# Masks and identity made on GpSimd, and a new order of steps, in a fused linear-attention and gated-MLP kernel

## The chip, the cores and the metric

The kernel runs on one core of one Trainium2 chip. The metric is the device time of one launch in microseconds (us), as the median of the runs shown. TensorE is called PE here, VectorE DVE, ScalarE ACT, GpSimd POOL, and SyncE SP; SP issues every transfer of this kernel.

## The reference

Gated linear attention over 768 tokens for 4 batches of 8 heads of 48 features, followed by a block with a spatial gating unit:

```python
f = 1.0 / (1.0 + np.exp(-f_logit))
for t in range(S):
    state = f[:, :, t, :, None] * state + np.einsum('bhd,bhe->bhde', k[:, :, t], v[:, :, t])
    y[:, :, t] = np.einsum('bhd,bhde->bhe', q[:, :, t], state)
x = y with the heads side by side                      # (4, 768, 384)
h = gelu_tanh(x @ w_in);  u, v = halves of h           # 512 columns each
v_n = (v - mean) / sqrt(var + 1e-6) * g_ln
v_s = np.einsum('ts,bsd->btd', w_sg, v_n) + b_sg[None, :, None]
out = x + (u * v_s) @ w_out
```

## The kernel before

The 3,072 tokens are 24 tiles of 128, six to a batch; three tiles are a group. Every step of a tile has a name and an engine, and a table, ORDER, lists all steps in one sequence. A name with `:DVE`, `:ACT` or `:POOL` behind it is put on that engine; without it the step goes to the first engine of its entry in T (line 41). The class Plan (line 148) walks ORDER with its own costs and sorts the steps by the start that it works out. The program is then written out in that sequence, and each engine runs its own steps in it, strictly one after the other.

The steps that the texts below name, for tile n:

- Loads on SP's queue: `f`, `q`, `k`, `v` (192 KB each), `ldin c` (384 KB of w_in, chunk c of 8), `cs` (the constants, 160 KB). At most eight loads are under way: each later one waits for the landing of the load eight before it.
- Gates: `e` and `l` (ACT, exp and log of f), `cum` (PE, a product with the triangle `tril` of the tile cs), `up` and `dn` (ACT, exp of plus and minus its result), `mq` and `mk` (q and k times these).
- Transposes: `tr` (PE, with `ident` of the tile cs), `tc n.0` and `tc n.1` (copies out of PSUM). `do`, `di`: the decays picked out and copied.
- Attention: `su` (PE, scores and state updates), `ms` (DVE, scores times `mask` of the tile cs), `sa` and `sm` (state added and multiplied), `w` (v shifted by 64 rows), `y` (PE), `ty` and `jy` (y out of PSUM and summed).
- The block: `xT` (PE, x transposed), `xh`, `xl` (its high and low parts), `hv` (PE, the v half of x @ w_in, which reads chunks 4 to 7), `hu` (PE, the u half, chunks 0 to 3), `gv`, `ns`, `nd`, `nq`, `nr`, `nh`, `nl` (the norm), `sg` (PE, the product with w_sg over six tiles), `po` (PE, w_out).
- A chunk of w_in comes as 64-bit floats and is turned into a high and a low part in eight steps: `wa` (ACT), `wp`, `wq`, `wr`, `wc` (DVE), `wd` (their sum), `we` (high part), `wf` (low part). `wd` and `wf` run on DVE or POOL.

POOL starts with `clear` (line 338), which sets the padding columns of the buffers for q, k and the decays. In the idle time that Plan expects on PE up to 45 us it places products of zeros (line 1042), which nothing reads.

Of the kernel before, what the change touches and what calls it, by code (L numbers as in the profile page):

```python
# [18 lines left out]
C = 64
# [48 lines left out]
wqin1 wcin6 mq0 mk0 wrin1 tr0 do0 cum1 tc0.0 tc0.1:DVE w0.1 wcin1 di0 wdin1 up1 dn1 wein1 wain4 w0.0:ACT mq1 su0 ms0
mk1 wdin6 wpin4 wqin4 wrin4 sa0.0 sm0.0 sa0.1 do1 tr1 y0 ldin7 f2 v1 f3 ldin5 q2 k2 f4 q3 f5 v2 k3 tc1.1 wein6 tc1.0
wain7 sm0.1 wcin4 di1 wpin7 ty0 e2 l2 w1.1 jy0 wqin7 su1 xT0 cum2 e3 l3 wain5 xh0 up2 dn2 sa1.0 ms1 wrin7 w1.0 wcin7  # L70
wpin5 wdin7 mq2 xl0 mk2 wfin1:POOL wfin6:POOL wdin4:POOL sm1.0:POOL cum3 y1 do2 tr2 up3 dn3 wein7 ty1 e4 di2:ACT l4
tc2.1 tc2.0 wfin7:POOL one sa1.1 jy1 wqin5 mq3 wein4:DVE wrin5 ldin0 g v3 ldsg2 ldsg1 q4 ldin2 b k4 xT1 cum4 do3 su2
xh1 e5 wcin5 l5 di3 wdin5 xl1 mk3 cum5 tr3 wein5 up4 dn4 wfin5 up5 dn5 tc3.0 w2.0:ACT tc3.1 wain0 ms2 sm1.1 sa2.0
sm2.0 sa2.1 wpin0 wqin0 sm2.1 wrin0 wcin0 w2.1:ACT wfin4:POOL hv1 su3 y2 wT2.0 wT1.0 hv0 gv1 ty2 wh2.0 sa3.0 ns1 ms3
jy2 xT2 wh1.0 nd1 wain2 nq1 xh2 wl1.0 wl2.0 mk4 wpin2 wdin0:POOL sm3.0:POOL sa3.1 xl2 mq4:POOL nr1 gv0 v4 q5 k5 f6
ldsg0 ldin3 v5 bb0 do4 tr4 ns0 wein0:DVE bc0 di4 nh1 tc4.0 tc4.1 w3.1:POOL nl1 mq5 w3.0 wqin2 wT2.1 hv2 y3 su4 wh2.1
nd0:DVE w4.0:ACT gv2 e6 ty3 mk5 wl2.1 wrin2 sm3.1 wcin2 ns2 sa4.0 ms4 w4.1:POOL sm4.0:POOL wdin2:POOL tr5 wT0.0 do5
jy3 sa4.1 sm4.1:POOL w5.1:POOL tc5.1 tc5.0:DVE wain3 wh0.0 xT3 y4 su5 wT0.1 wl0.0 wpin3 w5.0 xh3 wein2 ty4 nd2 wh0.1
nq2 nq0 wqin3 jy4 wfin2 di5 xl3 sa5.0 wrin3 wl0.1 cum_c ms5 hu0.1 xT4 l6 xh4 nr2 sm5.0:POOL wcin3 xl4 sz6 nr0 hu0.2
bb1 y5 hv3 ldout3 q7 ldout1 v7 q6 k6 ldout2 v6 f7 ldsg4 k7 v8 k8 f8 waout1 waout3 bc1 nh0 wpout3 wpout1 lh6:DVE wqout1  # L80
wdin3 nl0 ty5 gu0.1 gu0.2 gv3 jy5 wfin0:POOL wqout3 wrout1 ns3 wcout1 wein3:DVE wdout1 weout1:DVE wrout3 xT5 hu0.0 hv4
wT1.1 xh5 nd3 nq3 nh2 ll6:POOL xl5 nl2 wcout3 nr3 zr waout2 nh3 w6.0:ACT wdout3 hv5 nl3 wpout2 gv4 gu0.0 wh1.1 gv5
w8.0:ACT wfin3 ns4 wl1.1 ns5 nd5:DVE wfout1 wqout2 wrout2 nd4 nq4 nq5 nr4 nr5 hu1.1 cum6 hu1.2 hu1.0 gu1.1 gu1.2
wcout2 nh4:DVE nl4 nh5:DVE wdout2:POOL nl5 hu0.3 hu1.3 up6 dn6 e7 e8 mq6:POOL mk6 tt6.0 weout3 weout2 l7 tt6.1 wfout3
lh7:DVE wfout2:POOL ll7 gu1.3 gu0.3 gu1.0 sg0.0 ldsg3 ldsg5 q8 f9 to6 do6 ti6.0 ti6.1 ti6.3 ti6.2 ldout0 di6.0 di6.1
f10 cum7 wT4.0 wT3.0 sb0.0 e9 l8 up7 l9 wh4.0 wh3.0 dn7 sm_0.0:POOL mq7:POOL wl4.0 wl3.0 sg0.2 wT4.1 wT3.1 sg0.3 lh8
wh3.1 wh4.1 sb0.2 mk7 wl3.1 wl4.1 tt7.0 sm_0.2:POOL ll8:POOL tt7.1 tc6.1:DVE sh0.2:DVE tc6.0 cum8 wT5.1 wT5.0 su6
sl0.2 sb0.3 wh5.0 wh5.1 up8 sh0.0:DVE sm_0.3 lh9:DVE dn8 e10 w6.1:ACT waout0 ll9:POOL mk8:POOL wl5.1 sa6.0 wl5.0
wpout0 wqout0 mq8 do7 to7 f11 ti7.1 ti7.0 di7.1 q9 k9 ti7.2 ti7.3 sg0.1 cum9 sg1.2 sg1.0 sb0.1 wrout0 sm6.0 tt8.0
wcout0 tt8.1 sl0.0 sm_0.1:POOL e11 sh0.1 up9 l10 dn9 lh10:DVE sl0.1 w7.0 wdout0 weout0 ms6 w7.1:POOL ll10:POOL  # L90
sh0.3:DVE sa6.1 tc7.1 tc7.0 sl0.3 mq9 sb1.0 mk9 wfout0:POOL cum10 y6 su7 po1 po0 to8 do8 f12 di7.0 ti8.1 ti8.2 ti8.3
k10 ti8.0 v9 tt9.0 up10 l11 e12 ty6 dn10 sm6.1:POOL jy6 tt9.1 sa7.0 sb1.2 ms7 sm7.0:POOL sm_1.0 sa7.1 mk10 re0 w9.1
lh11:DVE sm7.1:POOL ll11 tc8.1 tc8.0 xT6 y7 su8 po2 cum11 do9 to9 di8.1 q10 di8.0 out0 ti9.3 ti9.0 ti9.2 ti9.1 ty7 xh6
xl6 ms8 jy7 sm_1.2 sa8.0 w8.1:POOL re1 sm8.0 mq10 sa8.1 tt10.0 tt10.1 sh1.2:DVE sh1.0:DVE up11 dn11 tc9.1 tc9.0 sl1.2
di9.1 v10 q11 k11 do10 f13 hv6 y8 su9 xT7 sg1.1 w10.1:ACT l12 ty8 xh7 jy8 xl7 mk11 gv6 lh12 sm8.1:POOL mq11:POOL re2
tt11.0 ns6 tt11.1 ll12:POOL to10 v11 di9.0 out1 f14 ti10.2 ti10.1 do11 ti10.3 ti10.0 to11 di10.1 k12 q12 xT8 sg1.3
cum12 xh8 e13 w10.0:ACT l13 lh13 up12 e14 ms9 sa9.0 xl8 sb1.1 sm_1.1 sh1.1:DVE sl1.0 sm9.0 sb1.3 sa9.1 w9.0:POOL
w11.0:POOL l14 nd6 tc10.0 dn12 w11.1 tc10.1:DVE sm_1.3 ll13 sh1.3:DVE hu2.1 hv8 su10 y9 cum13 ti11.3 ti11.1 k13 di11.0
ti11.2 di10.0 ti11.0 nq6 gv8 gu2.1 mk12 sl1.1 ns8 sl1.3 tt12.0 nr6 sm9.1:POOL mq12 tt12.1 ms10 nd8 up13 dn13 sa10.0
sm10.0 sa10.1 ty9 nh6 nl6 jy9 tc11.0 tc11.1 to12 q13 di11.1 ti12.3 ti12.1 ti12.0 v12 ti12.2 hv7 hu2.0 po3 su11 y10  # L100
hu2.2 gv7 re3 sm10.1 mk13 ns7 nd7:DVE nq7 lh14 sa11.0 tt13.0 sm11.0:POOL ll14:POOL ty10 jy10 gu2.2 nq8 gu2.0 ms11 mq13
tc12.0:DVE tc12.1:DVE nr7 nr8 xT9 hu2.3 xT10 cum14 y11 su12 xh9 gu2.3 xh10 nh8 ty11 xl10 xl9 tt13.1 jy11 nh7:DVE nl7
hv10 xT11 po4 do13 k14 to13 f15 do12 f16 ti13.1 ti13.2 out3 ti13.0 ti13.3 v14 v13 f17 di12.1 di12.0 di13.1 q14 k15 q15
out2 gv10 xh11 up14 dn14 ns10 nd10:DVE re4 nl8 xl11 hv9 hu3.1 hv11 hu3.2 nq10 e15 w12.0:ACT l15 nr10 mk14:POOL sz12
nh10:DVE lh15:DVE gv9 gu3.1 ll15 tt14.0 w12.1 ns9 nl10 nd9 gv11 ns11 nd11:DVE nq11 nq9 gu3.2 nr11 nr9 ms12 sa12.0
sm12.0 w13.0:ACT tc13.1 sa12.1 tc13.0:DVE hu3.0 po5 cum15 y12 su13 hu3.3 nh9 up15 dn15 e16 gu3.0 gu3.3 l16 lh16 e17
ty12 re5 nl9 nh11:DVE nl11 sg2.2 mk15 tt15.0 ms13 w14.0:ACT l17 w13.1:ACT sm12.1:POOL mq15:POOL sb2.2 mq14 tt14.1
sm_2.2 sh2.2:DVE jy12 ll16:POOL out5 do15 q16 v15 di15.0 di13.0 f18 to14 ti14.1 ti14.0 do14 ti14.2 ti14.3 k16 f19
sg2.1 cum16 xT12 sg2.0 xh12 lh17 e18 up16 dn16 sb2.0 sl2.2 sm_2.0 tt15.1 mq16:POOL ll17:POOL sb2.1 sa13.0 tc14.1 sh2.0
sl2.0 sm13.0 xl12 sg2.3 cum17 sg3.1 hv12 sm_2.1:POOL w14.1:POOL mk16:POOL sb2.3 sh2.1 up17 tc14.0 e19 l19 dn17 sl2.1  # L110
tt16.0 tt16.1 sa13.1 do16 to15 ti15.0 ti15.1 out4 to16 ti15.2 ti15.3 di14.0 f20 di15.1 di14.1 y13 su14 sg3.0
sm13.1:POOL sm_2.3:POOL ty13 gv12 sh2.3 w15.1:ACT sa14.0 ms14 w15.0:ACT jy13 sl2.3 tc15.1:DVE sb3.0 tc15.0:DVE sm14.0
po7 xT13 po6 e20 l20 l18 lh18 xh13 re7 sb3.1 sa14.1 xl13 ll18:POOL sm14.1:POOL y14 su15 hv13 cum18 po8 q17 ti16.3 k17
di16.1 ti16.0 ti16.1 out7 ti16.2 v16 ty14 tc16.1 lh19 sa15.0 ms15 mq17:POOL re6 mk17 sm15.0:POOL sm_3.0 tt17.0 up18
dn18 sh3.0 gv13 tt17.1 jy14 tc16.0:DVE sa15.1 y15 su16 sg3.2 xT14 do17 v17 k18 q18 out6 to17 ti17.2 f21 ti17.3 ti17.1
di16.0 ti17.0 mq18 ms16 mk18:POOL sg3.3 xh14 e21 tc17.0 ty15 w17.1:POOL sm_3.1:POOL sm15.1 ns13 re8 sa16.0 ns12
# [1045 lines left out]
```

## Time and profile before

| what | us |
|---|---|
| median of 3 runs (364.12 to 364.65) | 364.22 |
| the profiled execution, its own time | 364.64 |
| its span, first to last instruction | 362.9 |
| PE busy | 351.8 (97%) |
| DVE busy | 246.3 (68%) |
| ACT busy | 211.4 (58%) |
| POOL busy | 97.3 (27%) |

The busy time of PE holds the products of zeros of the first 32 us, and its busy share is an average: from about 34 us on it is full, and what is idle lies before that and in the last 5 us. The span and the execution's own time differ by 1.7 us that lie outside the recorded instructions. The granted clock of TensorE was 0.999 over the span.

### The profile page before, as it was taken

The numbers are of one execution on the slowest core, as the hardware profiler recorded it, in microseconds if no ns is written. First come the engines' busy times: TensorE is split into PE (matmuls) and PEld (weight loads), VectorE is DVE, ScalarE is ACT, GpSimd is POOL, SyncE is SP. The second block draws the span as 40 slices with busy tenths as digits, with TensorE's granted clock in tenths as the row PEclk, the third lists the DMA queues.
The fourth block names the chain that finished last, engine by engine and source line by source line (L and its number), as shares of the span: only waits on it lengthen the run. The fifth ranks groups of instructions, "written<-read, shape, count | busy, mean of one in ns | idle before, by whom it ended". The sixth has DMA issues, their size and how long they took to land.

```text
span 362.9 us, 11340 instructions
## 1 busy us (share of the span) xinstructions
PE 351.8 (97%) x4670; PEld 323.2 (89%) x4670; DVE 246.3 (68%) x559; ACT 211.4 (58%) x458; POOL 97.3 (27%) x154
## 2 busy tenths in 40 slices
...
GB/s 176 230 181 261 201 121 227 179 48 173 155 141 209 160 174 98 211 113 116 139 150 216 83 142 52 137 100 129 81 89 90 198 112 2 2 22 2 0 43 95
DMA packets 134047, 45.90 MB, mean 126 GB/s; under 512 B 117221, under 2 KB 130405, under 8 KB 133990
## 3 DMA queue, kind: packets, MB, share of 16 engines
...
q8 instruction: 38, 0.62, 0.8%
q14 instruction: 19, 0.16, 0.1%
...
## 4 chain that ended last, share of the span: by engine, by line
PE 81%; DVE 10%; DMA 2%; ACT 2%; issue 2%; SPq 1%; DVEq 0%
PE ps_b L664 64%; PE ps_y L640 5%; PE ps_s L592 3%; PE ps_b L669 2%; PE ps_s L597 2%; DMA gg<-in_moe_w_in_dram 2%; PE ps_b L547 1%; PE ps_b L1042 1%; DMA raw<-kq_d 1%; DVE st L602 1%; PE ps_b L498 1%; PE ps_b L424 1%; DVE vs L303 1%; PE ps_b L499 1%; DVE x L648 1%
## 5 line engine op out<-in xcount | busy, mean ns | idle before, releaser
L664 PE MATMUL ps_b<-w_sg_hi,vh 128*128 128x384 f32 x192 | 65.8, 343 | 0.0
L664 PE MATMUL ps_b<-w_sg_hi,vh_lo 128*128 128x384 f32 x192 | 64.9, 338 | 0.0
L664 PE MATMUL ps_b<-w_sg_lo,vh 128*128 128x384 f32 x192 | 64.8, 338 | 0.0
L664 PE MATMUL ps_b<-w_out_hi,gg 128*128 128x384 f32 x174 | 48.4, 340 | 0.0
L757 DVE SCALAR_TENSOR_TENSOR tmp<-ps_b,cols,b_bc 128x384 f32<-128x384 f32 x32 | 19.4, 609 | 26.1 <-PE ps_b L664 25.4
L664 PEld LDWEIGHTS ps_b<-w_sg_hi,vh 128*128 128x128 f32 x192 | 36.1, 188 | 0.2
L664 PEld LDWEIGHTS ps_b<-w_sg_lo,vh 128*128 128x128 f32 x192 | 36.1, 188 | 0.0
L664 PEld LDWEIGHTS ps_b<-w_sg_hi,vh_lo 128*128 128x128 f32 x192 | 36.0, 188 | 0.0
L296 ACT ACT_TABLE_LOAD x25 | 32.1, 1283 | 0.4
L664 PEld LDWEIGHTS ps_b<-w_out_hi,gg 128*128 128x128 f32 x174 | 31.7, 188 | 0.2
L762 POOL TENSOR_TENSOR tmp<-tmp,u 128x384 f32<-128x384 f32 x15 | 16.5, 1097 | 48.3 <-DVE tmp L757 40.2
L640 PEld LDWEIGHTS ps_y<-vs,st 64*64 64x64 f32 x768 | 24.5, 134 | 5.2 <-issue 3.7
L664 PE MATMUL ps_b<-w_out_lo,gg 128*128 128x384 f32 x87 | 29.1, 335 | 0.0
L664 PE MATMUL ps_b<-xTh,w_in_hi 128*128 128x384 f32 x84 | 28.9, 344 | 0.0
L664 PE MATMUL ps_b<-xTl,w_in_hi 128*128 128x384 f32 x84 | 28.4, 338 | 0.0
L664 PE MATMUL ps_b<-xTh,w_in_lo 128*128 128x384 f32 x84 | 28.3, 337 | 0.0
L640 PE MATMUL ps_y<-vs,st 64*64 64x48 f32 x768 | 27.4, 220 | 0.0
L640 PE MATMUL ps_y<-S,sk 48*64 48x48 f32 x768 | 27.2, 220 | 0.0
L298 ACT ACTIVATE f<-f 128x384 f32<-128x384 f32 x48 | 24.7, 523 | 2.3 <-DMA f<-in_f_logit_dram 1.8
L718 POOL TENSOR_SCALAR vg_rs<-vg_mv 128x1 f32<-128x1 f32 x24 | 5.1, 213 | 77.4 <-ACT vh_lo L714 72.9
L664 PE MATMUL ps_b<-w_in_hi,xTh 128*128 128x512 f32 x63 | 25.6, 407 | 0.0
L664 PE MATMUL ps_b<-w_in_hi,xTl 128*128 128x512 f32 x63 | 24.9, 395 | 0.0
(144 smaller groups left out, 891.4 us busy)
## 6 DMA issues: line engine op xcount, KB each, us to landing
...
```

The costliest lines, as they stand in the source:

```text
L296: nc.scalar.preload_act_table_set(SETS[want])
L298: nc.scalar.activation(dst, src, func, **kw)
L303: (nc.scalar.copy if e == "ACT" else ENG[e].tensor_copy)(dst, src)
L424: nc.tensor.transpose(ps[:, j], t[:, (hf * KT + j) * P : (hf * KT + j + 1) * P], ident)
L592: nc.tensor.matmul(ps_s[rows(score_rows(c, 2 * p + par)), par, p * C : (p + 1) * C], sk[r, 0, p, c], sk[r, 1, p, c], start=True, stop=True)
L597: nc.tensor.matmul(ps_s[feat(par), c, 256 + p * D : 256 + (p + 1) * D], kt[rows(c), h], vs[rows(c), h], start=True, stop=True)
L640: nc.tensor.matmul(ps_y[rows(c), half, h * D : (h + 1) * D], a, m, start=start, stop=stop)
L664: nc.tensor.matmul(ps, a, m, start=(j == 0), stop=(j == len(seq) - 1))
L669: nc.tensor.transpose(ps[:, j], x_sb[n][:, j * P : (j + 1) * P], ident)
L718: nc.gpsimd.tensor_scalar(rs, mv[:, 1:2], 1.0 / FH, 1e-6, op0=ALU.mult, op1=ALU.add)
L757: nc.vector.scalar_tensor_tensor(t, psum[f"sg{g}.{ft}"][:, :E], g_col[:, ft : ft + 1], b_bc[:, tokens(g)], op0=ALU.mult, op1=ALU.add)
L762: ENG[e].tensor_mul(t, t, uT.pop((g, ft)))
```

## The change

The tile cs is no longer loaded. Seven POOL instructions at the start of the program make the three constants in it: the triangle, the identity and the mask (an AFFINE_SELECT keeps or fills an element by its row and column). SP's queue loses one load. ORDER is a new sequence over the whole program, with other engines for some steps, and one constant of Plan, by which it expects loads between 20 and 65 us to land late, goes from 0.55 to 0.1.

```diff
 T = dict(
-    cum_c="DVE:0.2", clear="POOL:1.3", zy="DVE:0.6", ...
+    cs="POOL:2.0", cum_c="DVE:0.2", clear="POOL:1.3", zy="DVE:0.6", ...
...
-sz0 clear f0 ldin6 ldin1 cs q0 f1 k0 e0 wain6 l0 v0 q1 ldin4 k1 cum0 wain1 up0 dn0 e1 l1 zs zy wpin6 wqin6 wpin1 wrin6
+f0 ldin6 ldin1 cs clear f1 q0 k0 e0 l0 wain6 zy zs wpin6 wqin6 v0 q1 k1 ldin4 ldin7 v1 f2 cum0 f3 wain1 up0 dn0 e1
...
-    LATE = (20.0, 65.0, 0.55)
+    LATE = (20.0, 65.0, 0.1)
...
+    def make_consts():
+        pool = nc.gpsimd
+        pool.memset(tril, -1.0)
+        pool.affine_select(out=tril, in_=tril, compare_op=ALU.is_ge, fill=0.0, base=0, pattern=[[1, P]], channel_multiplier=-1)
+        pool.memset(tril[:C, C:], 0.0)
+        pool.memset(ident, 0.0)
+        pool.affine_select(out=ident, in_=ident, compare_op=ALU.not_equal, fill=1.0, base=0, pattern=[[-1, P]], channel_multiplier=1)
+        for c in range(2):
+            r = slice(c * C, (c + 1) * C)
+            pool.tensor_scalar(mask[r], tril[r, r], -1.0, None, op0=ALU.mult)
+
...
-    dma("cs", lambda e: nc.sync.dma_start(cs, cst), W["cs"], ())
+    op("cs", lambda e: make_consts(), T["cs"], (), due=-9.0)
```

Line numbers of the changed kernel are 12 higher behind the new function. Three places of the sequence follow.

**ACT, its first steps.** A number behind a name tells buffers apart (gg_123 and u_135 belong to chunk 6 before). Before, from the exponential of the first gate tile: e0, wa of chunk 6, l0, wa of chunk 1, up0, dn0, e1, l1, then a copy of tr0.

```order
L298 ACTIVATE f_112,flag_e_87<-f_112 128x384
L377 ACTIVATE u_135<-gg_123 128x384
L298 ACTIVATE f_112<-f_112 128x384
L377 ACTIVATE u_146<-gg_125 128x384
L298 ACTIVATE eb0_102<-ps_b0_67 128x8x48
L298 ACTIVATE f_112<-ps_b0_67 128x384
L298 ACTIVATE f_129,flag_e_87<-f_129 128x384
L298 ACTIVATE f_129<-f_129 128x384
L303 COPY sk0_96<-ps_b1_68 112x512
```

Now:

```order
L299 ACTIVATE f_121,flag_e_87<-f_121 128x384
L299 ACTIVATE f_121<-f_121 128x384
L389 ACTIVATE u_144<-gg_123 128x384
L389 ACTIVATE u_151<-gg_126 128x384
L299 ACTIVATE eb0_102<-ps_b0_67 128x8x48
L299 ACTIVATE f_121<-ps_b0_67 128x384
L299 ACTIVATE f_128,flag_e_87<-f_128 128x384
L304 CAST w_in_hi1_76<-u_144 128x3x128
L299 ACTIVATE f_128<-f_128 128x384
L299 ACTIVATE eb1_103<-ps_b1_68 128x8x48
L304 COPY sk0_96<-ps_b3_70 112x512
```

l0 has moved ahead of both wa steps, and `we` of chunk 6 (the CAST) now stands between e1 and l1. On PE, cum1 has moved ahead of tr0.

**POOL, its first 128x384 steps.** Before: wf of chunks 1 and 6, wd of chunk 4, sm1.0, wf of chunk 7, a small fill, wf of chunk 4.

```order
L415 TENSOR_TENSOR w_in_lo0_77<-u_146,w_in_hi0_75 128x3x128
L415 TENSOR_TENSOR w_in_lo1_78<-u_135,w_in_hi1_76 128x3x128
L399 TENSOR_TENSOR u_239<-u_239,u_240 128x384
L621 TENSOR_TENSOR S1_101<-S1_101,dec_106 112x192
L415 TENSOR_TENSOR w_in_lo1_78<-u_301,w_in_hi1_76 128x3x128
L900 MEMSET raw_99 1x128
L415 TENSOR_TENSOR w_in_lo1_78<-u_239,w_in_hi1_76 128x3x128
```

Now: mq0, the small fill, wd of chunk 1, wf of chunk 6, mk1, the state's zero, sm1.0, wd of chunks 7 and 5, wf of chunk 7.

```order
L529 TENSOR_TENSOR kq0_90<-kq0_90,eb0_102 128x8x48
L912 MEMSET raw_99 1x128
L411 TENSOR_TENSOR u_151<-u_151,u_152 128x384
L427 TENSOR_TENSOR w_in_lo1_78<-u_144,w_in_hi1_76 128x3x128
L524 TENSOR_TENSOR kq1_91<-kq1_91,f_128 128x8x48
L989 MEMSET S0_100 112x192
L633 TENSOR_TENSOR S1_101<-S1_101,dec_106 112x192
L411 TENSOR_TENSOR u_299<-u_299,u_300 128x384
L411 TENSOR_TENSOR u_370<-u_370,u_371 128x384
L427 TENSOR_TENSOR w_in_lo1_78<-u_299,w_in_hi1_76 128x3x128
```

Five steps of this size stood on POOL ahead of hv1, and now seven do; wf of chunk 1 comes later, and wf of chunk 4 is on DVE.

**DVE, the steps around wd of chunk 7.** Before, wd of chunk 7 (L399) stands on DVE between wp of chunk 5 and mq2:

```order
L394 SCALAR_TENSOR_TENSOR u_302<-gg_144,u_302 128x384
L382 TENSOR_SCALAR u_365<-u_365 128x384
L399 TENSOR_TENSOR u_301<-u_301,u_302 128x384
L517 TENSOR_TENSOR kq2_92<-kq2_92,eb0_102 128x8x48
L689 TENSOR_TENSOR w_sg_hi1_80<-ps_b0_67,w_sg_hi1_80 128x3x128
L512 TENSOR_TENSOR kq2_92<-kq2_92,f_149 128x8x48
```

Now wc of chunk 7 (the first row) is followed by jy0 and ms1, which read PSUM, and further down wc of chunk 5 is followed by jy1 and xl0, which read PSUM too:

```order
L406 SCALAR_TENSOR_TENSOR u_300<-gg_161,u_300 128x384
L660 SCALAR_TENSOR_TENSOR x_355,flag_y_88<-ps_y_72,x_355 128x384
L614 TENSOR_TENSOR st_98<-ps_s_71,cs_73 128x512
L394 TENSOR_SCALAR u_370<-u_370 128x384
L398 SCALAR_TENSOR_TENSOR u_370<-gg_176,u_370 128x384
L529 TENSOR_TENSOR kq2_92<-kq2_92,eb0_102 128x8x48
L402 TENSOR_SCALAR u_371<-u_370 128x384
L524 TENSOR_TENSOR kq2_92<-kq2_92,f_168 128x8x48
L406 SCALAR_TENSOR_TENSOR u_371<-gg_176,u_371 128x384
L660 SCALAR_TENSOR_TENSOR x_423,flag_y_88<-ps_y_72,x_423 128x384
L701 TENSOR_TENSOR w_sg_hi1_80<-ps_b2_69,w_sg_hi1_80 128x3x128
```

The wd steps of chunks 7 and 5, which DVE thereby loses, are the two with u_299 and u_370 on POOL above. On PE the same 215 units follow from hv1 to the end, in a sequence that differs in places.

## Rows read from the trace of the kernel before

**Rows 1.** Busy time of each engine in three stretches, us from the span's start.

```profile
20.00:30.00 10.00, 8.71 (x212) 6.78 (x204) 9.88 (x23) 8.05 (x22) 3.42 (x5) 1.00 0.99 185
30.00:40.00 10.00, 10.00 (x231) 7.84 (x231) 9.05 (x22) 9.22 (x22) 2.00 (x3) 1.00 1.09 232
100.00:150.00 50.00, 49.89 (x957) 45.91 (x956) 40.03 (x97) 36.51 (x76) 10.74 (x19) 1.00 0.71 164
```

The columns are the stretch, its length, busy time of PE, PE's weight loads, DVE, ACT and POOL with their instructions, PE's granted clock, the busy share of the 16 DMA engines, and GB/s.

**Rows 2.** Timeline of PE: start, duration, engine, line, operation, tiles, count, [idle before].

```profile
8.39 0.88 PE L495 MATMUL ps_b<-f,cs 128*128 128x384 f32 x2 [2.78 <-ACT u L377]
...
12.12 1.04 PE L547 MATMUL ps_b<-cs,kq 128*112 128x128 f32 x8
...
34.64 0.47 PE L664 MATMUL ps_b<-w_in_hi,w_sg_hi 128*128 128x512 f32 x1
...
62.11 0.55 PE L669 MATMUL ps_b<-cs,x 128*128 128x128 f32 x3 [0.44 <-DVE x L648]
...
76.83 0.34 PE L664 MATMUL ps_b<-w_sg_hi,vh 128*128 128x384 f32 x1
77.01 0.33 PE L664 MATMUL ps_b<-w_sg_lo,vh 128*128 128x384 f32 x1
```

**Rows 3.** Timeline of ACT, 6 to 8 us.

```profile
6.59 0.54 ACT L377 ACTIVATE u<-gg 128x384 f32<-128x384 f32 x1 [2.18 <-DMA gg<-in_moe_w_in_dram]
7.04 0.51 ACT L298 ACTIVATE f<-f 128x384 f32<-128x384 f32 x1
7.72 0.55 ACT L377 ACTIVATE u<-gg 128x384 f32<-128x384 f32 x1 [0.18 <-DMA gg<-in_moe_w_in_dram]
```

**Rows 4.** Timeline of SP's queue: the load of the constants.

```profile
2.49 0.49 SPq L891 DMA_DIRECT2D cs<-in_consts_dram  x1
```

**Rows 5.** Timeline of POOL.

```profile
0.72 0.26 POOL L977 MEMSET S<- 112x192 f32 x1 [0.29 <-POOLq L1145]
...
2.13 0.10 POOL L344 MEMSET cols<- 128x1 f32 x1
...
30.80 1.00 POOL L415 TENSOR_TENSOR w_in_lo<-u,w_in_hi 128x384 fp32r<-128x384 f32 x1 [2.58 <-DVE w_in_hi L303]
...
73.68 1.09 POOL L399 TENSOR_TENSOR u<-u 128x384 f32<-128x384 f32 x1
```

**Rows 6.** Timeline of DVE.

```profile
15.74 0.68 DVE L602 TENSOR_TENSOR st<-ps_s,cs 128x512 f32<-128x512 f32 x1
16.34 1.06 DVE L512 TENSOR_TENSOR kq<-kq,f 128x384 f32<-128x384 f32 x1
...
17.80 0.35 DVE L382 TENSOR_SCALAR u<-u 128x384 uint32<-128x384 uint32 x1
...
19.82 1.06 DVE L621 TENSOR_TENSOR S<-S,dec 112x192 f32<-112x192 f32 x1
...
21.72 0.94 DVE L303 COPY vs<-vs 64x192 f32<-64x192 f32 x1
...
25.66 0.35 DVE L382 TENSOR_SCALAR u<-u 128x384 uint32<-128x384 uint32 x1
25.93 0.55 DVE L399 TENSOR_TENSOR u<-u 128x384 f32<-128x384 f32 x1
26.39 0.55 DVE L517 TENSOR_TENSOR kq<-kq,eb 128x384 f32<-128x384 f32 x1
...
27.33 1.18 DVE L512 TENSOR_TENSOR kq<-kq,f 128x384 f32<-128x384 f32 x1
...
30.96 1.26 DVE L394 SCALAR_TENSOR_TENSOR u<-gg,u 128x384 f32<-128x384 uint32 x1
...
33.66 0.55 DVE L415 TENSOR_TENSOR w_in_lo<-u,w_in_hi 128x384 fp32r<-128x384 f32 x1
...
73.82 1.24 DVE L723 TENSOR_SCALAR vh<-vg,vg_rs 128x512 fp32r<-128x512 f32 x1
...
75.17 1.31 DVE L730 SCALAR_TENSOR_TENSOR vh_lo<-vg,vg_rs,vh 128x512 fp32r<-128x512 f32 x1
```

155 lines of the change are left out of this document (78 added, 77 removed).

## Prediction

> **What bounds the kernel now.** I read first the busy time by stretches, then the timeline of PE around the places where it waits, then POOL and DVE before those places.
>
> From 30 to 40 us PE is busy for the whole 10 us, and from 100 to 150 us for 49.89 of 50, both at a granted clock of 1.00 [rows 1]. From hv1 at 34.64 us on it is a continuous stream of products to the last po; the wait in front of xT5 at 62.11 us, 0.44 us for jy5 on DVE, is the longest that I found in it [rows 2]. So the end of the launch is hv1's start, plus a fixed amount of PE work, plus what PE is made to wait. Ahead of hv1 PE does not set the pace: 2.78 us of idle stand before cum0 alone [rows 2], and products of zeros fill most of the rest. There DVE is the bound: 9.88 us busy of 10 between 20 and 30 us, against 3.42 on POOL [rows 1].
>
> Part of that busy time on DVE is no work. In an unbroken run a step that reads a 128x384 tile takes 0.46 to 0.48 us from start to start (I take 0.47) and a short one 0.27 (the starts at 25.66, 25.93 and 26.39) [rows 6]. But sm0.1 at 19.82 and w1.1 at 21.72, short steps of some 0.35 us, took 1.06 and 0.94, and mk2 at 27.33 and wc of chunk 5 at 30.96 took 1.18 and 1.26 instead of 0.55 [rows 6]. Each began just behind a POOL step of 1.0 us (that at 30.80 is one of the four) and ended when that had ended [rows 5]. mk1 at 16.34 is a fifth. ms0 at 15.74 ran beside such a POOL step too and took its usual 0.68; it reads PSUM [rows 6]. So a POOL step on two tiles holds a DVE step that reads only SBUF for 0.6 to 0.7 us, and one that reads PSUM not at all.
>
> **The change, part by part.**
>
> *The constants.* SP's queue loses one issue of 0.49 us [rows 4] and the queue 160 KB. The two w_in chunks of 384 KB arrived at 6.59 and 7.72 us [rows 3], that is 384 KB in 1.13 us, so cs took some 0.47 us of transfer; by the 185 GB/s of 20 to 30 us [rows 1] it would be 0.9. All loads behind it come 0.5 us earlier (0.47 to 0.9). Chunks 6 and 1 stood ahead of it and come no earlier, and DVE begins with them. POOL now makes the tile. The trace has no AFFINE_SELECT: from below I take the fill of 0.26 us, from above the 1.0 us of a step on two tiles three times as wide [rows 5]. Two of these and five small steps of 0.1 to 0.26 are 1.2 to 3.0 us; I take 2. `clear` follows, which ended at 2.23 us [rows 5] and so will end at about 4 (3.4 to 5.2). The triangle, ready by 3 us, is wanted by cum0 at 5. So this costs nothing, hidden in POOL's idle start; mq0 on POOL is the first that would be late, and it can't begin before 9.
>
> *The first products.* l0 ran at 7.04 us, behind wa of chunk 6, which waited for its load until 6.59 [rows 3]. Put ahead of that it can run at 4.4, and cum0 at 5 instead of 8.39. But up0 stays behind wa of chunk 1, which ends at 8.27 [rows 3]: it gains 1.0 us, no more. From there step by step, with the durations above. mq0 on POOL runs 9.05 to 10.05 and holds wq of chunk 1 on DVE. wd of chunk 6 ends near 11.0; `we` of chunk 6 on ACT waits for it, and l1 is queued behind that, so l1 ends at 12.0, cum1 runs at 12.05, and tr0, now behind cum1 on PE, at 12.9 instead of 12.12 [rows 2]. This order costs 0.8 us at tr0. It is won back at once: cum1 is already done, so up1 and dn1 are 1.7 us earlier, su0 comes at 14.6 and ms0 at 15.65 (before 15.74). Now sa0.0, sa0.1 and sm0.1 follow directly, and wp of chunk 4 starts at 17.25 instead of 17.80 [rows 6], with those three (0.8 us) already behind it and with mk1 done on POOL.
>
> *DVE from wp of chunk 4 to hv1's last input.* Before, this ran from 17.80 to the end of wf of chunk 5, 33.66 + 0.47 = 34.13: 16.33 us. In it are 13 short steps (13 x 0.27 = 3.5), 18 of 0.47 (8.46) and ms1 (0.60, from 15.74 to 16.34): 12.57. The four holds are 0.71 + 0.59 + 0.63 + 0.71 = 2.64. The rest, 1.1, are two small copies and gaps between steps that depend on each other. In the changed order the stretch ends with wf of chunk 4 and has 8 short steps (2.16), 18 of 0.47 (8.46), ms1 and tc2.0 (1.2) and the copy cum_c (0.2): 12.0. Of the holds little should be left: wd of chunk 7 on POOL starts when wc of chunk 7 ends, and DVE is then at jy0 and ms1; wd of chunk 5 meets jy1 and xl0; wf of chunk 7 meets sa1.1 and xl1. All of these read PSUM. I take 0.2, and 1.0 again for the gaps: 17.25 + 12.0 + 0.2 + 1.0 = 30.45. hv1 follows mk3, tr3 and this wf, at about 31.2 us instead of 34.64. That is a floor: every wait in this walk was counted at its shortest. If all seven POOL steps held DVE for 0.65 us, the sum would be 3.2 us longer and hv1 at 34.4. I take 32.0, nearer the floor, because the places beside PSUM steps follow from the order: 2.6 us gained.
>
> *From hv1 to the end.* The same 215 units stand on PE; I cost their new order at nothing. What can take back the gain is DVE at sg0.0. Before, nl5 ended at 75.17 + 1.24 = 76.41 [rows 6]; its readers are the last three of the 18 products of sg0.0, which begin 0.18 us apart from 76.83 [rows 2], so the 16th at 79.5. The slack is 3.1 us. Now nl4 comes last, read from the 13th product on, 0.5 us sooner: that leaves 2.6. DVE has by then much the same steps to do, but two of the holds there (nh5 at 73.82, 1.24 us, and nl5, 1.31, beside POOL's steps from 73.68 on [rows 5, 6]) go, since those two POOL steps move to DVE: 1.4 us of holds for 0.94 of work. So 2.5 to 3 us pass through here, with nothing to spare. For this and for waits like the 0.44 at xT5 I take off 0.6. The last po and the three stores behind it are as before.
>
> The sum: -2.6 + 0.6 = -2.0 us on the profiled execution's own 364.64, so 362.6; the median of the runs is 0.42 below that execution, so **362.2**.
>
> **The rivals.** About 0.2% (0.7 us) is what a measurement of this kernel can tell from no change.
>
> *Faster as above* (360.8 to 363.4): needs the holds gone and sg0.0 on time.
>
> *POOL holds DVE as before.* Seven POOL steps of 1.0 us stand ahead of hv1 where five stood. Start times shift by tenths, and a step that was to meet jy0 may meet wp. For it: five of five such steps held DVE before. Against it: ms0 was not held, and the new neighbours read PSUM. With 7 x 0.65 = 4.55 us of holds, less the 1.35 that I counted (0.85 at wq, 0.3 at mq1, 0.2 later), hv1 comes at 31.2 + 3.2 = 34.4; with the 0.6 at sg0.0 the time is about 364.6. The Trainium skill ("SBUF — State Buffer", section "Who interferes with whom") says that DVE and POOL share one port pair, that a DVE instruction with two SBUF inputs contends with a POOL instruction that reads SBUF, and that one with at most one SBUF input does not, outside the two-port modes. The five holds and ms0 agree with that. By its words alone every further POOL step is a risk to DVE, and this rival is what it would make of the change wherever the neighbours slip.
>
> *The loads become the bound.* From 30 to 40 us the DMA engines are at a share of 1.09 [rows 1]. If k3 or chunk 5 arrives only when it did before less 0.5 us, and compute is ahead by 3, PE gets only 0.5 to 1: 363.5. Against it: in this stretch DVE's steps were not seen to wait for a load.
>
> *Slower: the constants are late.* If one AFFINE_SELECT takes more than about 3.2 us, `clear` ends after 9, mq0 starts late, and with it tr0 and everything to hv1, by 2 us for each us more. At 4.6 us the gain of 2.0 has gone and 0.8 is lost: 365.0. Nothing in the trace speaks for such a price; nothing measures it.
>
> **How the numbers follow.** Faster as above 0.64; holds as before 0.20; loads 0.07; late constants or, likewise, DVE so late at sg0.0 that all is lost 0.09. Faster by over 0.2%: 0.62 of the first and 0.03 of the loads, 0.65. Same: 0.02, 0.13 of the holds and 0.04, 0.19. Slower: 0.07 of the holds and 0.09, 0.16. The range goes from the floor of the walk with nothing taken off (hv1 at 31.2, -3.4: 360.8) to the holds with a little more (364.9).
>
> **What would show it.** Right: hv1 between 31 and 33 us; DVE steps of 0.9 us and more nearly gone before it; cum0 near 5; nl4 ending shortly before its reader, PE with no wait over 1 us behind hv1. Wrong: long DVE steps beside POOL's 1.0 us steps again; DVE or ACT waiting for loads between 15 and 30 us; PE idle before tr0 or at sg0.0; AFFINE_SELECT over 3 us.

## The result, and the profile after

The changed kernel takes 360.68 us (median of 13 runs, 360.13 to 363.58) where before took 364.12 in the same series (363.51 to 366.44). The ratio is 0.9915 with a 95% interval from 0.9892 to 0.9937: faster by 3.1 us, 2.3 to 3.9. I had forecast 362.2, from 360.8 to 364.9. The median lies 0.1 us below that range; the ratio put on the 364.22 of the prediction gives 361.1, inside it. The direction was right, the gain one and a half times what I gave. The profiled execution took 360.64 us with a span of 358.9, 4.0 less than before's own 364.64 and 362.9. Executions of one and the same kernel differ by some 3 us here, and the longer ones show a lower mean granted clock; a trace is one execution, so its times stand beside the medians and not in their place.

Busy time by stretches of the changed kernel, in the columns of [rows 1]:

```profile
20.00:30.00 10.00, 10.00 (x175) 7.46 (x174) 9.68 (x24) 8.95 (x26) 4.12 (x5) 1.00 1.00 186
30.00:40.00 10.00, 10.00 (x176) 8.06 (x175) 8.56 (x21) 8.24 (x19) 4.72 (x8) 1.00 1.04 236
100.00:150.00 50.00, 49.70 (x837) 45.75 (x836) 38.14 (x90) 37.43 (x79) 10.25 (x18) 1.00 0.74 167
```

DVE is still the busiest engine from 20 to 30 us, and POOL has more to do. Between 100 and 150 us PE lost 0.19 us more than before. PE's timeline, which answers to [rows 2]:

```profile
5.15 0.88 PE L507 MATMUL ps_b<-f,cs 128*128 128x384 f32 x2 [0.25 <-ACT f L299]
5.87 3.82 PE L1054 MATMUL ps_b<-zeros 128*128 128x512 f32 x10
9.89 0.91 PE L507 MATMUL ps_b<-f,cs 128*128 128x384 f32 x2 [0.20 <-ACT f L299]
10.64 1.06 PE L559 MATMUL ps_b<-cs,kq 128*112 128x128 f32 x8
...
29.93 1.04 PE L559 MATMUL ps_b<-cs,kq 128*112 128x128 f32 x8
30.72 0.48 PE L676 MATMUL ps_b<-w_in_hi,w_sg_hi 128*128 128x512 f32 x1
...
60.01 0.49 PE L681 MATMUL ps_b<-cs,x 128*128 128x128 f32 x3
...
75.25 0.34 PE L676 MATMUL ps_b<-w_sg_hi,vh_lo 128*128 128x384 f32 x1
...
123.27 0.34 PE L604 MATMUL ps_s<-sk 48*64 48x64 f32 x8 [0.22 <-ACT sk L304]
```

cum0 runs at 5.15 instead of 8.39, hv1 at 30.72 instead of 34.64. From hv1 to the end of the last po it is 323.13 us (30.72 to 353.85), before 323.07. So in this execution all of the gain was made ahead of hv1, and all of it reached the end. The wait at xT5 (now at 60.01) is gone; a new one, 0.22, stands at su10. The two wa steps on ACT, which answer to [rows 3], show when chunks 6 and 1 landed:

```profile
5.20 0.55 ACT L389 ACTIVATE u<-gg 128x384 f32<-128x384 f32 x1 [0.20 <-DMA gg<-in_moe_w_in_dram]
6.51 0.56 ACT L389 ACTIVATE u<-gg 128x384 f32<-128x384 f32 x1 [0.76 <-DMA gg<-in_moe_w_in_dram]
```

DVE and POOL on the way to hv1, which answer to [rows 6] and [rows 5], are:

```profile
5.79 0.36 DVE L394 TENSOR_SCALAR u<-u 128x384 uint32<-128x384 uint32 x1 [3.46 <-ACT u L389]
...
12.24 1.24 DVE L529 TENSOR_TENSOR kq<-kq,eb 128x384 f32<-128x384 f32 x1 [0.25 <-DMA kq<-in_q_dram]
...
15.46 0.35 DVE L394 TENSOR_SCALAR u<-u 128x384 uint32<-128x384 uint32 x1
...
19.73 0.35 DVE L630 TENSOR_TENSOR S<-S,ps_s 112x192 f32<-112x192 f32 x1 [0.86 <-PE ps_s L609]
...
20.95 0.69 DVE L614 TENSOR_TENSOR st<-ps_s,cs 128x512 f32<-128x512 f32 x1
21.55 0.55 DVE L394 TENSOR_SCALAR u<-u 128x384 uint32<-128x384 uint32 x1
...
24.55 0.55 DVE L660 SCALAR_TENSOR_TENSOR x<-ps_y,x 128x384 f32<-128x384 f32 x1
...
25.02 0.55 DVE L701 TENSOR_TENSOR w_sg_hi<-ps_b,w_sg_hi 128x384 fp32r<-128x384 f32 x1
25.49 0.65 DVE L529 TENSOR_TENSOR kq<-kq,eb 128x384 f32<-128x384 f32 x1
...
29.25 0.55 DVE L427 TENSOR_TENSOR w_in_lo<-u,w_in_hi 128x384 fp32r<-128x384 f32 x1
...
71.42 0.75 DVE L742 SCALAR_TENSOR_TENSOR vh_lo<-vg,vg_rs,vh 128x512 fp32r<-128x512 f32 x1
```

```profile
1.08 0.29 POOL L342 TENSOR_SCALAR_AFFINE_SELECT cs<-cs 128x128 f32<-128x128 f32 x1
...
4.13 0.10 POOL L356 MEMSET cols<- 128x1 f32 x1
8.82 1.19 POOL L529 TENSOR_TENSOR kq<-kq,eb 128x384 f32<-128x384 f32 x1 [4.59 <-DMA kq<-in_q_dram]
...
12.07 0.99 POOL L427 TENSOR_TENSOR w_in_lo<-u,w_in_hi 128x384 fp32r<-128x384 f32 x1
13.33 1.03 POOL L524 TENSOR_TENSOR kq<-kq,f 128x384 f32<-128x384 f32 x1 [0.26 <-DMA kq<-in_k_dram]
...
20.88 1.00 POOL L411 TENSOR_TENSOR u<-u 128x384 f32<-128x384 f32 x1
24.71 1.01 POOL L411 TENSOR_TENSOR u<-u 128x384 f32<-128x384 f32 x1 [2.83 <-DVE u L406]
26.28 1.00 POOL L427 TENSOR_TENSOR w_in_lo<-u,w_in_hi 128x384 fp32r<-128x384 f32 x1 [0.56 <-ACT w_in_hi L304]
```

One DVE step is still held for long: mq1 at 12.24 (1.24 us), begun behind wf of chunk 6 on POOL (12.07). Two more are held for the rest of a POOL step: wp of chunk 5 at 21.55 takes 0.55 instead of 0.35 (POOL's step ends at 21.88), and mq3 at 25.49 takes 0.65 instead of 0.55 (POOL's ends at 25.72). The steps that read PSUM are not held though they begin behind POOL's: ms1 at 20.95, behind wd of chunk 7 (20.88), takes 0.69, and xl0 at 25.02, behind wd of chunk 5 (24.71), takes 0.55. jy1 at 24.55 takes its usual 0.55 too, but it began ahead of POOL's step. So had ms0 in the kernel before (15.74, POOL's step at 15.99); these two alone would not show that a reader of PSUM is free.

Taking as held what a step takes beyond 0.55 (two inputs of 128x384), 0.35 (short ones) or 0.25 (copies of vs), DVE's way from its first chunk step to hv1's last input divides so: before 52 steps in 27.05 us, 3.25 held, 2.15 idle, 21.65 work; after 47 steps in 24.01 us (5.79 to 29.80), 0.99 held, 2.08 idle, 20.94 work. Of the 3.04 us saved 2.26 are holds and 0.71 is work that DVE no longer has. DVE also began 1.37 us sooner; why is the subject of several runs. Against that, hv1 stood 0.92 us behind DVE's last input instead of 0.43: tr3 ran at 29.93, behind cum5 on PE, though mk3 had ended at 29.33. Together 3.04 + 1.37 - 0.49 = 3.92 us at hv1.

### The profile page after: what moved, and what is told of

It reads as the page before. It is cut to its first block, busy times and chain, and to the rows that moved or that the text cites. A ratio compares the mean times of both kernels' runs of the same rounds, so it can differ in the third digit from the quotient of the medians.

```text
span 358.9 us, 11336 instructions
## 1 busy us (share of the span) xinstructions
PE 351.7 (98%) x4664; PEld 322.9 (90%) x4664; DVE 243.5 (68%) x553; ACT 213.7 (60%) x469; POOL 98.9 (28%) x158
## 4 chain that ended last, share of the span: by engine, by line
PE 87%; DMA 5%; DVE 3%; SPq 2%; ACT 1%; issue 1%
PE ps_b L676 65%; PE ps_y L652 6%; PE ps_s L604 4%; DMA raw<-kq_d 3%; PE ps_s L609 2%; PE ps_b L681 2%; PE ps_b L559 2%; PE ps_b L544 1%; PE ps_b L436 1%; PE ps_b L1054 1%; DMA kq_d<-gg 1%; DMA gg<-in_moe_w_in_dram 1%; PE ps_b L507 1%; PE ps_b L510 1%; PE ps_b L511 1%
## 5 line engine op out<-in xcount | busy, mean ns | idle before, releaser
L774 POOL TENSOR_TENSOR tmp<-tmp,u 128x384 f32<-128x384 f32 x13 | 14.1, 1088 | 49.6 <-DVE tmp L769 37.2
L633 POOL TENSOR_TENSOR S<-S,dec 112x192 f32<-112x192 f32 x22 | 12.5, 570 | 45.8 <-DVE S L630 34.2
L604 PEld LDWEIGHTS ps_s<-sk 48*64 48x64 f32 x768 | 20.8, 133 | 4.8 <-issue 2.1
```

The lines of the kernel that those rows point to most:

```text
L604: nc.tensor.matmul(ps_s[rows(score_rows(c, 2 * p + par)), par, p * C : (p + 1) * C], sk[r, 0, p, c], sk[r, 1, p, c], start=True, stop=True)
L633: ENG[e].tensor_mul(state_to(n, c), state_to(n, c), decay(n, c))
L774: ENG[e].tensor_mul(t, t, uT.pop((g, ft)))
```

## The experiments

The theory after the result: hv1 sets the end; the new order took away the holds; the load that was dropped had delayed the first chunks of w_in. Twelve runs follow, in three groups, each beside runs of before; the ratios are to these. Runs 1 and 10 are single executions, taken for their traces. A table of what the traces show stands behind the last experiment.

**1. The kernel before, again**, unchanged.

> The kernel before, unchanged, for a second trace. In its first trace chunk 6 of w_in landed at 6.57 us and chunk 1 at 7.70; after the change at 5.18 and 6.49, though both were issued ahead of the constants' load that was dropped. Theory (the dropped load is what delayed them): they land near 6.5 and 7.7 again, DVE begins with wp of chunk 6 near 7.2, hv1 near 34.6. Rival (a delay of that one execution): they land near 5.2 and 6.5, DVE begins near 5.8; hv1 then between 33.2 and 34.6. The five held DVE steps (0.9 us and more) are there in either case.

363.95 us. wa of chunk 6 began at 5.66 instead of 6.59, hv1 at 33.96; the five held steps were there (1.06, 1.06, 0.95, 1.18, 1.26). Where the first chunk lands differs between executions of the same kernel, and 0.9 us of it moved hv1 by 0.7.

**2. The constants alone.**

```
 T = dict(
...
+    cs="POOL:2.0", ...
...
+    def make_consts():
...
-    dma("cs", lambda e: nc.sync.dma_start(cs, cst), W["cs"], ())
+    op("cs", lambda e: make_consts(), T["cs"], (), due=-9.0)
```

> The order of before, with the constants made on GpSimd and their load dropped. Theory (the load delays chunks 6 and 1): DVE begins 1.3 us earlier, near 5.8, the five holds of 0.6 to 0.7 us stay, hv1 near 33.3 to 33.8, about 1 us (0.3%) faster than before. Rival (the new order alone carries the gain, and the first q and k loads set the early pace either way): hv1 within 0.5 us of 34.6, no difference that can be told.

363.79 us, ratio 0.9982 (0.9963 to 1.0001): some 0.7 us, 1.3 at most, and the interval holds no difference, too. hv1 came at 33.52, where the theory had it, and the five holds were unchanged.

**3. The order alone.** The same two lines the other way round, in the changed kernel.

> The changed order, with the constants loaded by a DMA at the place in SyncE's queue where before had it. Theory: the holds that are gone (2.4 us) and the 0.7 us less of DVE work stay gained, the 1.3 us at the start of DVE are lost: hv1 between 31.5 and 32.3, about 2.5 us (0.7%) faster than before. Rival (the order needs early constants): cum0 waits for the load until about 8, up0 and with it mq0 and tr0 come 1 to 2 us later, and hv1 comes at 33 or later, under 1.6 us faster than before.

361.5 us, ratio 0.9911 (0.9877 to 0.9944), as fast as the whole change. So the order carries the gain, and the constants on GpSimd are not needed for it. hv1 stood at 33.41 in the trace, where the rival had it. The traced execution took 362.64, and it tells something that neither theory had: cum0 came at 8.65, behind 2.16 us in which PE had nothing to do, and then PE's granted clock fell:

```profile
8.00:9.00 1.00, 0.35 (x1) 0.30 (x2) 0.96 (x3) 0.55 (x1) 0.00 (x0) 1.00 0.13 26
9.00:13.40 4.40, 4.40 (x8) 1.90 (x7) 3.99 (x8) 2.19 (x6) 1.91 (x3) 0.61 1.26 190
13.40:20.00 6.60, 6.60 (x163) 5.95 (x163) 4.04 (x10) 4.19 (x10) 2.65 (x4) 1.00 1.16 262
```

0.61 over 9.0 to 13.4 us is mostly the lower level, 1.2 GHz. What ran then were the products of zeros that fill PE between cum0 and cum1 (Plan had placed 6 instructions here, which took 4.14 us; in the change 10 took 3.82): they ended at 13.4, cum1 and tr0 stood behind them, and tr0 came at 14.07 although mk0 had ended at 12.26.

**4. Two holds put back.** In the changed kernel's order, on DVE alone:

```
-sa1.0 wcin7 jy0 ms1 ...  wcin5 jy1 xl0
+sa1.0 jy0 ms1 wcin7 ...  jy1 xl0 wcin5
```

> The changed kernel with four DVE steps moved by one or two places and nothing else: jy0 and ms1 ahead of wc of chunk 7, jy1 and xl0 ahead of wc of chunk 5. wd of chunk 7 and wd of chunk 5 on GpSimd, which wait for these two wc steps, then run beside steps that read only SBUF (wp and wq of chunk 5; mq3 and what follows) instead of steps that read PSUM. Theory (a GpSimd step on two SBUF tiles holds a DVE step that reads only SBUF): two DVE steps of 1.0 to 1.3 us appear where none was between 20 and 30 us, perhaps a third beside wf of chunk 7; DVE ends its work for hv1 0.9 to 1.9 us later, hv1 at 31.5 to 32.5, 0.2 to 0.5% slower than the changed kernel. Rival (holds have another cause, and the neighbour's source does not matter): no new step over 0.9 us, hv1 within 0.3 us of 30.72.

360.59 us, ratio 0.9895 (0.9867 to 0.9922): no slower than the change. DVE and POOL in its trace:

```profile
22.33 0.35 DVE L394 TENSOR_SCALAR u<-u 128x384 uint32<-128x384 uint32 x1
22.72 1.23 DVE L398 SCALAR_TENSOR_TENSOR u<-gg,u 128x384 uint32<-128x384 uint32 x1
...
26.56 0.55 DVE L529 TENSOR_TENSOR kq<-kq,eb 128x384 f32<-128x384 f32 x1
```

```profile
22.49 1.04 POOL L411 TENSOR_TENSOR u<-u 128x384 f32<-128x384 f32 x1 [0.97 <-DVE u L406]
26.72 1.25 POOL L411 TENSOR_TENSOR u<-u 128x384 f32<-128x384 f32 x1 [3.19 <-DVE u L406]
```

The first hold came as expected: wq of chunk 5 began at 22.72 behind POOL's step at 22.49 and took 1.23 where it took 0.56 in the changed kernel. The second did not: mq3 had begun 0.16 us ahead of POOL's step, kept its 0.55, and POOL's step took 1.25. Whoever begins first goes on, and the other waits. The Trainium skill ("SBUF — State Buffer", section "Who interferes with whom") says the same of the port pair that the two engines share: the order of issue decides who blocks. Both rows agree with it.

hv1 came at 32.07, inside what I expected, but mostly by luck: of the 1.35 us that it was later 0.80 is the landing of chunk 6 (wa at 6.00 instead of 5.20). DVE's stretch from wp of chunk 4 to hv1's last input took 14.65 us instead of 14.34, not the 0.9 us more that I gave as the least, since with the new hold the rests at wp of chunk 5 and mq3 went. The end was only 0.52 us later than the changed kernel's. So the experiment shows which step is held, and not what a hold costs in time.

**5. Two holds taken out of before.** w1.1 behind jy0; mk2, with do2, tr2, di2, l4, tc2.1 and tc2.0, behind jy1:

```
-w1.1 jy0 wqin7 ...  xl0 mk2 ... sa1.1 jy1
+jy0 w1.1 wqin7 ...  xl0 ... sa1.1 jy1 mk2
```

> The kernel before with two of its held steps moved behind steps that read PSUM, and nothing else: w1.1 behind jy0, and mk2 (with the products and copies that hang on it) behind sa1.1 and jy1. Theory (a GpSimd step on two SBUF tiles holds a DVE step that reads only SBUF and begins behind it): wd of chunk 4 and wf of chunk 7 on GpSimd then run beside jy0 and beside sa1.1 and jy1, two of the five DVE steps of 0.9 us and more vanish, DVE reaches hv1's last input up to 1.2 us sooner after ms0 than before (18.5 us in the first trace of before), and the time falls by 0.5 to 1.2 us (0.1 to 0.3%). Rival (the step that comes first is held whatever it reads): jy0 and jy1 or sa1.1 take 0.9 us or more instead, no gain.

365.48 us, ratio 0.9996 (0.9965 to 1.0028), no gain in the time, but in the trace the two holds were gone:

```profile
23.81 0.55 DVE L648 SCALAR_TENSOR_TENSOR x<-ps_y,x 128x384 f32<-128x384 f32 x1
...
24.40 0.47 DVE L303 COPY vs<-vs 64x192 f32<-64x192 f32 x1
...
29.79 0.56 DVE L512 TENSOR_TENSOR kq<-kq,f 128x384 f32<-128x384 f32 x1
```

jy0, begun 0.18 us behind POOL's step at 23.63, took 0.55, w1.1 behind it 0.47 (0.94 before), mk2 0.56 (1.18 before). From ms0 to the end of hv1's last input it was 17.5 us instead of 18.5: 1.0 us, near the expected 1.2. What ate it stands ahead of ms0. PE had waited 2.22 us for the constants' load, and behind cum0 the clock fell:

```profile
8.50:9.50 1.00, 0.60 (x2) 0.49 (x3) 0.82 (x3) 0.43 (x1) 0.00 (x0) 1.00 0.26 50
9.50:14.30 4.80, 4.80 (x9) 2.05 (x8) 2.33 (x6) 1.90 (x5) 0.00 (x0) 0.64 1.12 223
14.30:20.00 5.70, 5.31 (x98) 4.49 (x97) 4.54 (x10) 2.66 (x6) 1.00 (x1) 1.00 1.11 232
```

The filler in front of tr0 took 4.87 us instead of 3.17. Not every execution lost clock: five of the twelve had a mean granted clock of 0.996 or more and took 362.82 to 363.77 us, 362.97 in the median, where the 27 of 32 of before with such a clock took 363.97. That is 1.0 us less, inside the 0.5 to 1.2 expected. It sorts executions by what they showed, so it speaks for the worth of the two holds and does not prove it. Why seven of this kernel lost clock, and five of 32 of before, stays open.

**6. Two steps moved to bring hv1 sooner** in the changed kernel.

```
-w1.0:ACT e2 w1.1:ACT ... su2 cum5 ... tr3 hv1
+w1.0:ACT w1.1:ACT e2 ... su2 ... tr3 hv1 cum5
```

> The changed kernel with two steps moved: e2 behind w1.1 on ACT, cum5 behind hv1 on PE. In the changed kernel tr3 stood behind cum5 at 29.93 though mk3 had ended at 29.33. Theory: hv1 comes 0.5 to 0.8 us sooner behind mk3, but of that little reaches the end, because waits behind hv1 (0.37 at su4, 0.3 at su10, 0.13 at su12) give back 0.8 us whenever hv1 comes early: 0 to 0.5 us (0.1%) faster than the changed kernel. Rival (the end follows hv1 one to one): 0.5 to 0.8 us faster. The gap of 0.62 us inside su1 stays if PE's instruction fetch makes it, and goes if w1.1 does.

360.73 us, ratio 0.9907 (0.9879 to 0.9936), the same as the change. hv1 began at 30.42, 0.30 sooner, and the end came 0.24 sooner in this trace; the medians show nothing. But hv1 now has cum5, 0.64 us of PE work, behind it that stood ahead of it before, so counted from the same place PE was not sooner. The gap inside su1 was 0.35 us; it was 0.34 in experiment 10, where e2 stands where it stood, and there was none in experiment 12, which has this order. So the place of w1.1 does not make it.

**7. and 8. The constants made three and four times over**, `[make_consts() for _ in range(3)]`, and 4.

> The changed kernel with the seven GpSimd instructions that make the constants run three times over (6.2 instead of 2.07 us; the results are the same). Theory (the constants are hidden up to the first q, which lands near 8.7 and lets mq0 begin): the tile is ready at 7.0, cum0 follows at once instead of 5.15, clear ends near 8.4, mq0 begins within 0.4 us of q0's landing as before; the end moves by less than 0.4 us (0.1%). Rival (cum0's early start is what the gain rests on): tr0 and hv1 come 1 to 2 us later behind q0's landing, and the time is 1 us or more longer.

> The same four times over (8.3 us): the tile is ready near 9.1, clear ends near 10.5. Theory: cum0 at 9.2, up0 at 10.1, mq0 at 10.6 instead of 8.8, tr0 and hv1 some 1.7 us later; of that 0.8 us is met by the waits behind hv1 that are then not waited, so 0.5 to 1.2 us (0.1 to 0.3%) slower than the changed kernel. Rival (the end follows hv1 one to one): 1.7 us (0.5%) slower.

Three times: 361.54 us, ratio 0.9921 (0.9892 to 0.995), not told from the change; the interval holds no difference and 1 us too. Its trace is nearer the rival: tr0 at 13.14 and hv1 at 32.48, 1.35 us later behind the landing than in the change. cum0 began at 5.89, behind 0.99 us of idle time, and took 1.65 us instead of 0.88, and the filler behind it took 5.33 instead of 3.82, though the record of the granted clock stands at 1.00 there. So the early part was not as well covered as I said. Four times: 364.5 us, ratio 0.9996 (0.9969 to 1.0024), the whole gain gone, and more than either theory gave. PE's stretches and timeline of the kernel with four show why:

```profile
9.00:13.00 4.00, 3.98 (x6) 2.04 (x7) 1.83 (x4) 2.20 (x6) 3.71 (x13) 0.57 1.41 190
```

```profile
9.02 1.65 PE L507 MATMUL ps_b<-f,cs 128*128 128x384 f32 x2 [4.12 <-POOL cs L343]
10.46 4.81 PE L1054 MATMUL ps_b<-zeros 128*128 128x512 f32 x10
15.11 0.81 PE L507 MATMUL ps_b<-f,cs 128*128 128x384 f32 x2
15.76 1.04 PE L559 MATMUL ps_b<-cs,kq 128*112 128x128 f32 x8
```

cum0 came at 9.02 as expected. But the filler behind it is a fixed block in PE's order: it ran at the low clock after 4.12 us of idle time and put tr0 at 15.76, 5.1 us later than in the change, where I had counted 1.7.

**9. and 10. The old load beside the constants on GpSimd**, twice the same kernel; the tile it fills is not read before its own load.

```
-f0 ldin6 ldin1 cs clear ...
+f0 ldin6 ldin1 csd cs clear ...
...
+    dma("csd", lambda e: nc.sync.dma_start(vss[2].rearrange("p h d -> p (h d)")[:, :CW], cst), W["cs"], ())
```

> The changed kernel, with the constants made on GpSimd and used from there, and beside that the old 160 KB load issued again at its old place in SyncE's queue, into a tile that nothing reads before its own load. So far chunk 6 of w_in landed at 6.57, 5.63, 7.23 and 6.96 us in the four traces with this load and at 5.59, 5.18, 5.97, 5.36, 5.59 and 4.96 in the six without. Theory (the load holds up the chunks issued ahead of it): chunk 6 between 5.6 and 7.2, chunk 1 some 1.2 behind it, tr0 5.4 us behind chunk 6, hv1 25.5 behind it, at 31.2 to 32.7; 0.2 to 1.2 us (0.1 to 0.3%) slower than the changed kernel. Rival (chance): chunk 6 between 4.9 and 6.0, only the loads behind it 0.5 later, less than 0.5 us slower.

> The same kernel again, for a second trace of where chunk 6 lands: theory 5.6 to 7.2 us, rival 4.9 to 6.0.

360.63 us, ratio 0.9874 (0.9831 to 0.9918), and 360.1 for the single run: no slower than the change. wa of chunk 6 began at 7.02 in the one and 5.39 in the other, which is below the theory's 5.6. hv1 came at 32.16 and 31.15. Plan also placed a further block of zeros, some 0.43 us, between cum1 and tr0 here.

**11. A shorter filler in before**, two products of zeros between cum0 and tr0 instead of four.

```
-                if n < 1 or not k:
+                if n < 1 or not k or (s["name"] == "tr0" and t > last + 1.5):
```

> The kernel before with the products of zeros between cum0 and tr0 on PE cut from 2 x 512 + 512 + 256 columns to 2 x 512. In the trace of before tr0 ran at 12.12, behind the last of these, though mk0 had ended at 11.36. Theory (the filler sets tr0): tr0 at 11.4 to 11.5 if chunk 6 lands as in that trace, 5.0 instead of 5.6 us behind that landing, and hv1 0.5 to 0.7 us sooner; 0.1 to 0.2% faster. Rival 1 (DVE alone sets the pace to hv1): tr0 sooner, hv1 where it was behind chunk 6's landing (28.1), no gain. Rival 2 (the idle time costs PE its clock): a granted clock of 0.5 somewhere between 9 and 14 us, and 1 us or more slower.

364.47 us, ratio 0.9995 (0.9969 to 1.0021). tr0 ran as soon as mk0 had ended (11.41), behind 1.28 us of idle time. That is no gain: with the long filler and the same landing, experiment 1 had tr0 at 11.42. Two us later the clock fell, as rival 2 had it, though later than it said, and the medians do not show its loss of 1 us:

```profile
10.00:11.40 1.40, 0.13 (x1) 0.02 (x1) 0.70 (x2) 0.62 (x3) 0.00 (x0) 1.00 1.18 190
11.40:13.40 2.00, 1.99 (x17) 2.00 (x18) 1.00 (x3) 0.59 (x1) 0.00 (x0) 0.92 1.12 265
13.40:16.50 3.10, 3.10 (x67) 1.94 (x67) 1.86 (x6) 1.86 (x5) 0.53 (x1) 0.50 1.16 246
```

At 0.50 su0 took 1.85 us (1.09 before), and hv1 came 0.9 us later than in experiment 1 with the same landing.

**12. The waits behind hv1**, on top of experiment 6.

```
-y3 su4 ... tr5 bb1     ... hv8 su10 y9 ... cum13 hv7
+y3 bb1 su4 ... tr5     ... hv8 cum13 su10 y9 ... hv7
```

> The changed kernel with e2 behind w1.1 and cum5 behind hv1, as before, and two products moved into the waits behind hv1: bb1 between y3 and su4, cum13 ahead of su10. Theory (the wait of 0.37 in su4 is PE's instruction fetch running behind two units of 128 instructions each, that at su10 a copy that is late): 0.3 to 0.6 us less of waits behind hv1, and 0.3 us from hv1; 0.4 to 0.9 us (0.1 to 0.25%) faster than the changed kernel. Rival (the waits move on to the next unit): no difference.

360.92 us, ratio 0.9907 (0.9878 to 0.9936): the same. In the trace su4 took 1.09 us, where it had taken 1.42 in the change, but it took 1.06 in experiment 6 already, without bb1 ahead of it: this wait comes and goes between executions, and the run does not show that the move removed it. No version beat the change clear of noise.

What the fourteen traces show, in us: the start of wa of chunk 6 (the landing of the first chunk), hv1, the end of the last po, and the difference of the last two. In two rows, two steps moved and waits filled, cum5 stands behind hv1: take 0.64 off their last number to compare it.

```
                        load  wa6   hv1    end     end - hv1
before                  yes   6.59  34.64  357.71  323.07
before again            yes   5.66  33.96  356.93  322.97
before, constants only  no    5.62  33.52  356.50  322.98
before, two holds out   yes   7.25  35.86  358.77  322.91
before, short filler    yes   5.68  34.86  357.61  322.75
changed                 no    5.20  30.72  353.85  323.13
two steps moved         no    5.38  30.42  353.61  323.19
waits filled            no    6.03  30.81  353.87  323.06
load beside, 2nd trace  yes   5.39  31.15  353.52  322.37
two holds back          no    6.00  32.07  354.37  322.30
load beside             yes   7.02  32.16  354.48  322.32
constants x3            no    5.61  32.48  355.08  322.60
order only              yes   6.98  33.41  355.78  322.37
constants x4            no    4.99  35.10  357.39  322.29
```

## Why the prediction was right, and where it was off

*What bounds the kernel.* Right; hv1 at 30.72 even lies below the 31 to 33 that I named. In the order of before the end follows hv1 at 322.8 to 323.1 us. In the new order it follows at 322.3 to 322.6 as long as hv1 comes at 31.15 or later, and below that the end stays between 353.5 and 353.9. Two of these four traces are those with cum5 behind hv1, though; less its 0.64 they follow at 322.6 and 322.4. So that the end stops following rests on the changed kernel's own trace alone.

*The constants.* The sum of about 2 us was right (2.07), and so was the price between the fill and the two-tile step: 0.29 us for an AFFINE_SELECT, near the lower bound. `clear` ended at 4.23 (about 4 was said), cum0 ran at 5.15 (5). That they cost nothing is right as they are; four times their length took back the whole gain. The rival on late constants was right in its mechanism: its case of 365.0 had `clear` end at 11.8, four times the constants end it at 11.75, and the loss was 3.8 us by the medians (364.5 against 360.68) and 3.0 by the ratios to before (0.9996 and 0.9915), where the rival had 2.8. Its price, an AFFINE_SELECT of over 3 us, was far off.

*"Chunks 6 and 1 stood ahead of it and come no earlier"* is the step that failed. In this trace they came 1.4 and 1.2 us earlier, and together with a hold of 0.65 at wq of chunk 1 that did not happen (it had ended at 8.39, before mq0 began at 8.82) this brought tr0 to 10.64, where I had 12.9, and wp of chunk 4 to 15.46, where I had 17.25. Is it the load? With it, wa of chunk 6 began at 6.6 to 7.3 in four traces of seven and at 5.4 to 5.7 in three; without it at 5.0 to 6.0 in all seven. If the load had no part in it, four late ones would all fall on its side in 35 of 1001 ways. That speaks for the load, with a bound between late and early that was drawn after the fact, and shows that it isn't the load alone; how it delays a transfer issued ahead of it stays open. For the time it mattered little: the load put back beside the new order cost nothing that could be measured.

*The holds.* Right in the mechanism, and the largest part of what DVE saved: 2.26 of 3.04 us. The 0.99 that stayed answer to the 1.35 that I counted. That DVE at mq0 was not held was luck: the step in question (wr of chunk 1) began 0.04 us ahead of mq0, and in six of the nine traces in the new order a step there began behind it and took 1.18 to 1.38 us. The row that I built the rule for PSUM on, ms0, did not show it, since ms0 began ahead of POOL's step; ms1 and xl0 in the changed kernel and jy0 in experiment 5 do. Experiment 4 made one hold and experiment 5 removed two by moving DVE's steps past each other, with POOL's order left alone, but neither moved the median; in time the worth of the holds is seen only in the executions of experiment 5 that kept their clock. The rest of the new order (less work for DVE, earlier gates, cum1 ahead of tr0) was not run apart from the holds.

Compared at the same landing (hv1 less the start of wa of chunk 6: 28.05 before, 25.52 after) the change is worth 2.5 us at hv1, which is the 2.6 of the sum. The total was right by luck in its parts: wp of chunk 4 to hv1's last input took 14.34 us instead of the 13.2 of the floor. Its steps were the 12.0 that I counted and its holds 0.30 for 0.2, but its gaps were 2.0 for 1.0; 0.86 of that is idle time in front of sa1.0, whose products su1 on PE stood still for 0.62 us in the middle. The 0.8 that I put on the floor, thinking of holds, covered it.

*From hv1 to the end.* The 0.6 that I took off were 0.05 by the trace (323.13 against 323.07). sg0.0 was never near: nl4 ended at 72.17, and the first product that reads it, the 15th, ran at 75.25, 3.1 us of slack where I had said nothing to spare. The new order's stream is 0.7 us shorter than before's when nothing in it waits (the 0.44 at xT5 is part of that). Against it stand 0.8 us of waits in the changed kernel's trace: 0.37 in su4, 0.3 at su10, the rest at su12. At su10 it is ACT's copy of sk, behind a transfer:

```profile
122.08 1.14 ACT L304 COPY sk<-raw 112x512 f32<-112x512 f32 x2 [1.06 <-DMA raw<-kq_d]
```

So a transfer ends last there, which is all that came of the rival *loads become the bound*. It is a matter of this execution: in experiment 6 the same copies began at 120.94 and waited for no transfer.

*The sum*: -3.92 for -2.6 at hv1, +0.05 for +0.6 behind it, together -3.87 for -2.0. The 1.3 at hv1 is the landing in this execution (1.4). The 0.55 behind it is the part of the 0.6, taken off for sg0.0 and for waits, that was not needed. An estimate with the mean landings of all the traces (6.37 with the load, 5.55 without) is 2.5 + 0.8 = 3.3 us, near the 3.1 of the ratio, where the two single executions differ by 4.0. But the times do not bear out the 0.8: the order with the load (experiment 3) and the change with the load put back (9) were as fast as the change. How the 3.1 divides is open to that extent.

*What I overlooked.* In the first trace of before PE, not DVE, had set the pace ahead of tr0: mk0 ended at 11.36, and tr0 ran at 12.12 behind the products of zeros. In the second they ended in time, and tr0 ran at 11.42, as early as with the short filler. I called these filler and gave them no price. They have one on both sides: too long, they hold tr0 (experiments 3, 5, 8); too short, the clock falls (experiment 11).

What the constants on GpSimd add to the new order stays open within about 0.4%: alone they bring 0.2%, 0.4% at most, and without them the order is as fast.
